# A two-layer attention and FFN kernel whose beginning is laid out anew and whose second-layer rows are laid in pairs

## The chip, the core and the metric

The kernel runs on one core of a Trainium2 chip. The metric is the device time of one execution in microseconds (us). The engines are TensorE (PE, with its weight loads as PEld), VectorE (DVE), ScalarE (ACT), GpSimd (POOL) and SyncE (SP), which issues all DMA transfers here.

## The reference

```python
def _A_ref(x, wq, wk, wv, wo):            # H = 32 query heads, one key/value head, Dh = 16
    q = (x @ wq).reshape(B, S, H, Dh).transpose(0, 2, 1, 3)
    k = x @ wk
    v = x @ wv
    scores = jnp.einsum("bhqd,bkd->bhqk", q, k) * (Dh ** -0.5)
    p = softmax(scores, axis=-1)
    o = jnp.einsum("bhqk,bkd->bhqd", p, v)
    return o.transpose(0, 2, 1, 3).reshape(B, S, H * Dh) @ wo

def _B_ref(x, w1, w2):
    return jnp.maximum(x @ w1, 0) @ w2

for _ in range(2):                        # the same weights in both layers
    x = x + _A_ref(layernorm(x), wq, wk, wv, wo)
    x = x + _B_ref(layernorm(x), w1, w2)
```

x is 1 x 2048 x 512 in float32, w1 is 512 x 1792 and w2 is 1792 x 512. The layer norm has no gain and no offset.

## The kernel before, in words

The 2048 positions are four blocks of 512. The attention of a layer is cut into 32 units; a unit (U) is one block of 512 queries with four of the 32 heads, and runs over 16 tiles of 128 keys. One unit and one key tile make a step, so that both layers together have 1024 steps. A step is two pairs of score matmuls on PE (`scores`, L788, each with 64 of the 128 rows, two side by side), two exponentials on ACT of 128 x 1024 (L789), and eight value matmuls (`values`, L794). After its last tile a unit's sums are kept (L801, L803), stored, and read back in another layout (`unit_out` L810, `unit_sums` L817 and L819), inverted and spread through DRAM (`unit_inverse` L831, L833), and scaled (`unit_norm` L842).

The matrix products run on fp16 halves of float32 numbers: a product of two numbers is three products of high and low halves (`projection`, `mm3` L104; `batch` L125 uses 64 rows for two products side by side). A layer norm is L269 and L271 (statistics, DVE), L272 and L273 (variance to scale, POOL), L278 (apply, DVE); `halved` makes its fp16 high half on DVE (L287) and its low half on DVE or POOL (L288); `laid` transposes both by a DMA (L294) into a home, a tile that holds a block's 512 normed and transposed rows. `transposed` does the same on PE (L301).

`keys` (L315) makes the keys and values of one block: 12 products, a copy out of PSUM by `high` (L97 on ACT when the work is forced, L99 on DVE when not), two casts (L323), and the subtractions for the low parts on DVE and POOL (L325). The last block of a set also finds the key maximum, `key_norm`, whose row goes into the key tile by two DMAs (L355). `query` makes the queries of eight heads of one block (a group): it stores a high, a low and again a high half, for the upper and the lower 64 partitions each, into a DRAM buffer `qd` (L401). `squares` stores a row of squared lengths for every unit, in two DMAs a group (L381). `load_q` reads a unit's query tile from there (L749), and five such tiles turn over. The zero rows of the key and query tiles are written once, by ACT (L181) or POOL (L183).

All dense work besides the steps (norms, keys, queries, out-projection, FFN) stands in a queue of generators, each with a size and a step by which it is due. A planner, `timed`, walks through the 1024 steps with costs for scores, exponentials and values, and puts pieces of the first generator between them at a rate of size by steps left. A generator can yield ("lag", ..) to leave time for a result. `until` runs the queue at once until a condition holds: the work is then forced. `CHAINS` gives for each block the size and the due step of its out-projection and FFN. The first 32 steps take units 0 and 1 in turn, four key tiles each, so that key block b is needed from step 8b on. Layer 2 starts at step 512, and needs the keys of blocks 0 to 2 and the key maximum from there; its first ten units take tiles 12 to 15, those of block 3, in a second pass.

`start` (L410) normalises the first four tiles of rows and transposes them on PE, then makes the queries of group 0, then keys, then the squares. The other 12 tiles follow one at a time, laid by DMA, and block by block keys and a query group. `others` (L477) makes the queries of blocks 1, 2 and 3 later. In `chain` (L576) the down-projection of the FFN calls `finish` (L728) for each tile of 128 rows; for layer 1 it makes the norms for layer 2, and after all four the rows are laid together, followed by keys(1, b) and the list `fill` of query batches and squares that go into later gaps; `rest` (L706) empties that list.

## Time and profile before

| what | before |
|---|---|
| median of 3 runs | 2550.78 us (2549.84 to 2554.6) |
| profiled execution | 2550.61 us |
| its span | 2548.8 us |
| PE busy | 2376.9 us, 93% |
| ACT busy | 1974.4 us, 77% |
| DVE busy | 664.7 us, 26% |
| POOL busy | 241.1 us, 9% |
| mean granted TensorE clock | 0.977 |

In rows of groups of instructions, a line, an engine, an operation and the tiles (output <- input) are followed by the shapes, the count, the busy time in us, the mean in ns, and the idle time before them with what ended it. In rows of the timeline stand the start in us, the length, the engine, the line, the operation, the count of such instructions in a row, and in brackets the idle time before and what released it. SPq is a DMA issued by SP. A row of a stretch gives its limits and length, then the busy time and count of each engine.

### The profile page before, as it was taken

Reading aid. Unit: us, or ns where it says so; the run is one execution under the profiler, and the core shown is the slowest. Engines: PE = TensorE matmul, PEld = TensorE weight load, DVE = VectorE, ACT = ScalarE, POOL = GpSimd, SP = SyncE. Lnnn points to the kernel's source line nnn. Section 1 sums busy time; section 2 is a strip of 40 time slices with the busy share of each in tenths; the row PEclk is TensorE's granted clock in tenths of the full one; section 3 lists DMA queues with packets and bytes.
Section 4 is the critical chain, followed back from the end, with each engine's and each line's share of the span. In section 5 each row is a group of like instructions: output and inputs, shape, how many; then the busy total and the mean of one; then the engine's idle time right before and its main releaser. Section 6 shows DMA issues by size and latency. Waiting matters only on the chain.

```text
span 2548.8 us, 44836 instructions
## 1 busy us (share of the span) xinstructions
PE 2376.9 (93%) x18965; PEld 790.2 (31%) x18965; DVE 664.7 (26%) x1482; ACT 1974.4 (77%) x2090; POOL 241.1 (9%) x289
## 2 busy tenths in 40 slices
PE   5699999999999988999799998979999999999978
PEld 1122222333233323333133332223333333233334
DVE  4333322111421233222221122232123111221232
ACT  5489998888888876777588787868888888888720
POOL 3434520000100011000110000000000000000000
PEclk9899999999999999999899999999999999999989
DMA  3334432110321122210231112321122111121131
GB/s 105 91 112 152 127 113 69 57 58 17 94 90 57 41 78 54 95 54 30 73 87 40 44 38 65 122 82 57 41 71 74 53 57 54 54 71 44 35 117 64
DMA packets 168356, 180.78 MB, mean 71 GB/s; under 512 B 78956, under 2 KB 98684, under 8 KB 167632
## 3 DMA queue, kind: packets, MB, share of 16 engines
q1 hardware_dynamic: 168144, 177.81, 22.8%
q8 instruction: 150, 2.46, 0.4%
q14 instruction: 62, 0.51, 0.1%
HBM read 115.06 MB, written 47.97 MB: 64 GB/s over the span
## 4 chain that ended last, share of the span: by engine, by line
PE 77%; ACT 9%; DMA 4%; DVE 4%; issue 3%; POOL 2%; SPq 1%; ACTq 0%; POOLq 0%; DVEq 0%
PE facc L794 33%; PE fmisc L125 22%; PE fst L788 17%; ACT fp L789 8%; PE fmisc L104 4%; DMA fqd<-fqh 1%; DMA fod<-faccs 1%; DVE fxt L555 1%; DVE fbst L269 1%; SPq L401 1%; DMA flsum<-fod 1%; DMA frinv<-frd 0%; POOL fbmv L273 0%; POOL fxp L288 0%; DMA frd<-flsum 0%
## 5 line engine op out<-in xcount | busy, mean ns | idle before, releaser
L789 ACT ACTIVATE fp<-fst 128x1024 f32<-128x1024 f32 x2048 | 1943.8, 1029 | 420.2 <-PE fst L788 401.6
L794 PE MATMUL facc<-fp,fva 128*32 128x512 f32 x8192 | 1030.4, 605 | 5.1 <-DVE faccs L801 4.1
L788 PE MATMUL fst<-fqop,fkop 64*128 64x512 f16 x4096 | 790.2, 383 | 55.3 <-ACT fp L789 35.9
L788 PEld LDWEIGHTS <-fkop 64*128 64x128 f16 x4096 | 262.7, 93 | 865.7 <-issue 696.7
L794 PEld LDWEIGHTS facc<-fp,fva 128*32 128x32 f32 x8192 | 208.7, 108 | 411.0 <-issue 361.6
L125 PE MATMUL fmisc<-fw,fhh 64*128 64x512 f16 x1568 | 258.1, 376 | 5.4 <-DVE fseen L132 3.6
L555 DVE SCALAR_TENSOR_TENSOR fxt<-fmisc,fxt 128x512 f32<-128x512 f32 x156 | 102.5, 682 | 367.1 <-PE fmisc L125 343.8
L125 PE MATMUL fmisc<-fxt,fw 64*128 64x512 f16 x1344 | 188.2, 376 | 1.9 <-DMA fw<-fwd 0.8
L272 POOL TENSOR_SCALAR fbmv<-fbmv 128x1 f32<-128x1 f32 x64 | 17.8, 278 | 1782.2 <-DVE fbmv L271 1781.3
L132 DVE COPY fseen<-fmisc 1x1 f32<-1x1 f32 x266 | 28.4, 142 | 552.4 <-PE fmisc L125 552.1
L125 PEld LDWEIGHTS <-fw 64*128 64x128 f16 x2352 | 118.5, 94 | 128.5 <-issue 22.5
L125 PE MATMUL fmisc<-fxq,fw 64*128 64x512 f16 x1008 | 141.2, 377 | 11.5 <-DMA fxq<-fxp 11.0
L125 PE MATMUL fmisc<-fw,fhl 64*128 64x512 f16 x784 | 151.7, 376 | 0.0
L646 DVE TENSOR_SCALAR fhh<-fmisc 128x512 f16<-128x512 f32 x98 | 67.1, 685 | 295.1 <-PE fmisc L125 295.1
L125 PEld LDWEIGHTS <-fhh 64*128 64x128 f16 x1568 | 80.7, 94 | 78.9 <-issue 15.5
L801 DVE COPY faccs<-facc 128x512 f32<-128x512 f32 x64 | 44.2, 690 | 225.2 <-PE facc L794 225.2
L647 DVE SCALAR_TENSOR_TENSOR fhl<-fmisc,fhh 128x512 f16<-128x512 f32 x112 | 77.4, 691 | 35.3 <-ACT fhh L644 31.9
L125 PE MATMUL fmisc<-fwoh,fot 64*128 64x512 f16 x448 | 78.2, 376 | 2.5 <-DVE fseen L132 1.6
L516 POOL TENSOR_SCALAR faccs<-faccs 128x512 f32<-128x512 f32 x32 | 48.9, 1528 | 65.7 <-DVE fw L515 52.0
L125 PE MATMUL fmisc<-fxq,fwqh 64*128 64x512 f16 x320 | 52.9, 376 | 0.0
L397 POOL TENSOR_TENSOR fsq<-fqh 128x512 fp32r<-128x512 f16 x32 | 33.3, 1039 | 201.2 <-DVE fqh L99 195.2
L125 PEld LDWEIGHTS <-fhl 64*128 64x128 f16 x784 | 40.5, 94 | 36.1
(124 smaller groups left out, 995.7 us busy)
## 6 DMA issues: line engine op xcount, KB each, us to landing
fw<-fwd SPq DMA_DIRECT2D x224, 256.0 KB
fod<-faccs SPq DMA_DIRECT2D x64, 256.0 KB
fqop<-fqd SPq DMA_DIRECT2D x148, 98.0 KB
fxt<-in_A_x_dram SPq DMA_DIRECT2D x32, 256.0 KB
fqd<-fqh SPq DMA_DIRECT2D x128, 64.0 KB
foraw<-fod SPq DMA_DIRECT2D x32, 256.0 KB
frinv<-frd SPq DMA_DIRECT2D x32, 256.0 KB
faccs<-in_B_w_dram SPq DMA_DIRECT2D x28, 256.0 KB
```

The source lines that it names most:

```text
L104: self.nc.tensor.matmul(ps, a, b, start=(i == 0), stop=(i == n - 1))
L125: mm(ps[j], a[r], b[r], start=(turn == 0 and i == 0), stop=(turn == 1 and i == n - 1), skip_group_check=True)
L132: self.nc.vector.tensor_copy(self.wt("seen", [1, 1]), t[0:1, 0:1])
L397: nc.gpsimd.tensor_mul(sq[G], _f(qh), _f(qh))
L516: nc.gpsimd.tensor_scalar(raw, raw, self.ws, None, op0=MUL)
L555: self.nc.vector.scalar_tensor_tensor(xt, ps, 1.0 / factor, xt, op0=MUL, op1=ADD)
L646: nc.vector.tensor_scalar(hh, ps, 0.0, None, op0=MAX)
L647: nc.vector.scalar_tensor_tensor(hl, ps, 0.0, _f(hh), op0=MAX, op1=SUB)
L788: nc.tensor.matmul(st[:, hf], self.kop[U // 32][h, kt * P:(kt + 1) * P], q[h, pr, :], start=True, stop=True)
L789: nc.scalar.activation(p[:, 2 * pr:2 * pr + 2], st, AF.Exp, scale=self.up ** -2)
L794: self.nc.tensor.matmul(acc[32 * j:32 * j + 32], self.va[U // 32][:, kt], p[:, 2 * pr + hf], start=start, stop=stop, skip_group_check=True)
L801: self.nc.vector.tensor_copy(self.sums[U], acc)
```

## The change

1. `begin` takes the place of `start` for this path. Eight row tiles are loaded at the beginning, the last four behind the query weights. The order on PE is transposes of the rows, keys, the first query group, the key transposes and maximum, the squares. Zero rows are written by DVE; those of the later query tiles and of layer 2's key tile are put at step 5 (`remaining`).
2. The layer norms of tiles 4 to 7 stand right behind `begin`, those of tiles 8 to 15 at steps 1, 3, 7 and 9 (`rows`), in pairs and not one at a time; of each pair one low half is made on DVE, the other on POOL. Four homes hold the four blocks: xt2, xq2, ot2 and wo2, so that one block instead of two goes through DRAM (`xtd`). `following` then holds only keys and queries of blocks 1 to 3, and its keys are copied by DVE. `others` takes the blocks in the order 1, 3, 2; the out-projection weights, whose tile is a home now, come after that.
3. `qd` has another layout: `query` stores 3 tiles of 128 partitions in place of 6 of 64; `squares` stores all groups of a block with 2 DMAs in place of 8; a query load reads 49 x 2 x 512 in place of 49 x 1024 elements.
4. In layer 1 each pair of rows is laid in `finish`; the squares that are left in `fill` go before the last down-projection; for blocks 0 and 1 the first query batch follows the keys at once; the lag ahead of the keys is 8 throughout; the sizes and due steps of blocks 0 and 2 are other numbers.
5. The tile of the unit's outputs and of its spread inverse are double; units 33, 35 and 37 are scaled 14 steps behind and not 8.

```diff
-CHAINS = (((397, 272), (449, 400), (449, 508), (421, 626)), ((384, 784), (384, 912), (384, 1022), (384, 1152)))
+CHAINS = (((421, 272), (449, 400), (425, 500), (421, 626)), ((384, 784), (384, 912), (384, 1022), (384, 1152)))
...
             for h in (32, 96):
-                if early:
+                if not self.exact:
+                    self.nc.vector.memset(flat[h:h + 32], 0.0)
+                elif early:
...
-        r = 8 * len(groups)
-        nc.vector.tensor_scalar(qr[0:r], ps[0:r], 2 * SLACK / ONE, None, op0=MUL)
-        for i, G in enumerate(groups):
-            for pr in range(2):
-                nc.sync.dma_start(self.qd[L, b][2 * G:2 * G + 2, :, 48, pr, :].rearrange("u h q -> (u h) q"),
-                                  _f(qr)[8 * i + pr * 4:8 * i + pr * 4 + 4])
+        nc.vector.tensor_scalar(qr, ps[0:32], 2 * SLACK / ONE, None, op0=MUL)
+        n, G = 4 * len(groups), groups[0]
+        for pr in range(2):
+            dst = self.qd[L, b][G:G + len(groups), pr, :, :, 48].rearrange("g u h q -> g (u h) q")
+            nc.sync.dma_start(dst, _f(qr)[16 * pr:16 * pr + n])
...
-            for pr in range(2):
-                for c, t in ((0, qh), (1, ql), (2, qh)):
-                    dst = qd[2 * G:2 * G + 2].rearrange("u h (c d) p q -> c p (u h) d q", d=DH)[c, pr]
-                    nc.sync.dma_start(dst, _f(t)[64 * pr:64 * pr + 64])
+            for c, t in ((0, qh), (1, ql), (2, qh)):
+                dst = qd[G, :, :, :, c * DH:(c + 1) * DH].rearrange("p u h d q -> (p u h) d q")
+                nc.sync.dma_start(dst, _f(t))
...
+    def begin(self):
...
+        st = {t: self.stats(self.xin[t]) for t in range(2)}
+        xn = {0: self.apply(*st[0])}
+        self.prep_wkv(kraw)
+        for t in range(4):
+            if t < 2:
+                st[t + 2] = self.stats(self.xin[t + 2])
+            if t < 3:
+                xn[t + 1] = self.apply(*st[t + 1])
+            yield from self.transposed(xn[t], t, self.xt2)
+            self.load_x(t + 8)
+        self.prep_wq(qraw)
...
+        keys = self.keys(0, 0, self.xt2)
+        for w in keys:
+            yield w
+            if isinstance(w, tuple):
+                break
+        queries, squares = self.in_parts(0, 0, [0], self.xt2)
+        yield from queries
+        yield from keys
+        yield from squares
+
+    def rows(self, n):
+        while self.row < n:
+            todo, t = [], self.row
+            self.row += 2
+            for r in (t, t + 1):
+                self.ln(self.xin[r], r, todo)
+            for xp, r in todo:
+                self.laid(xp, r % 4, self.homes()[r // 4])
...
+    def remaining(self):
+        self.zero_rows(self.qop[2:] + [self.kop[1]])
+        self.fixed_rows(self.qop[2:] + [self.kop[1]])
+        self.nc.gpsimd.memset(self.va[1], self.vs / self.os)
+
+    def following(self):
+        yield ("lag", 1, 0.0, 9.0)
+        for b in range(1, NB):
+            self.rows(4 * b + 4)
+            yield from self.keys(0, b, self.homes()[b])
+            if b == 2:
+                self.nc.sync.dma_start(self.xtd, self.ot2[2])
+            yield from self.queries(0, 0, [b])
...
+        if L == 0 and b < NB - 1 and not self.exact:
+            yield from self.rest(fill)
+            fill = []
         yield from down(ready)
...
-            to = self.xq2 if b < NB - 1 else self.xt2
-            if b < NB - 1:
-                yield from self.rest(fill)
-                fill = []
-            for xp, r in self.todo:
-                self.laid(xp, r, to)
-            self.todo.clear()
-            yield ("lag", 1, 0.0, 4.0 if 0 < b < NB - 1 else 8.0)
-            yield from self.keys(1, b, to)
-            self.fill = fill + self.in_parts(1, b, range(4), to)
+            yield ("lag", 1, 0.0, 8.0)
+            yield from self.keys(1, b, self.row_home(b))
+            self.fill = fill + self.in_parts(1, b, range(4), self.row_home(b))
+            if b < 2:
+                yield from self.fill.pop(0)
...
             self.ln(xt, s, self.todo)
+            if s % 2:
+                for xp, r in self.todo:
+                    self.laid(xp, r, self.row_home(b))
+                self.todo.clear()
...
+            self.until(lambda: not self.gens)
+            self.rows(8)
+            self.add(self.following(), 80, 24)
             self.add(self.others(), 156, 142)
-            self.until(lambda: self.tile_no >= 5)
...
+            for i, t in ((1, 10), (3, 12), (7, 14), (9, 16)):
+                at(i, self.rows, t)
+            at(5, self.remaining)
...
-                    inverse, norm = (3, 6) if U == 31 else (5, 8) if 32 < U < 40 else (7, 12) if U % 8 == 7 else (9, 14)
+                    inverse, norm = (3, 6) if U == 31 else (7, 12) if U % 8 == 7 else (9, 14)
```

Three places show the instructions' order. The first is SP's queue at the beginning, from the first query stores (fqd) to the last key row; fqop are query tiles, fkop_75 is layer 1's key tile, fqr a row of squares or of the key maximum. Before:

```order
L401 DMA fqd_94<-fqh 4x16x512
L401 DMA fqd_94<-fql 4x16x512
L401 DMA fqd_94<-fqh 4x16x512 x2
L401 DMA fqd_94<-fql 4x16x512
L401 DMA fqd_94<-fqh 4x16x512
L381 DMA fqd_94<-fqr 4x512 x2
L749 DMA fqop_88<-fqd_94 49x1024 x2
L749 DMA fqop_89<-fqd_94 49x1024 x2
L355 DMA fkop_75<-fqr 1x4x512 x2
```

And of the change:

```order
L403 DMA fqd_93<-fqh 8x16x512
L403 DMA fqd_93<-fql 8x16x512
L403 DMA fqd_93<-fqh 8x16x512
L359 DMA fkop_75<-fqr 1x4x512 x2
L385 DMA fqd_93<-fqr 4x512 x2
L822 DMA fqop_87<-fqd_93 49x2x512 x2
L822 DMA fqop_88<-fqd_93 49x2x512 x2
L298 DMA_TRANSPOSE fxq<-fxp 128x8x128 x2
```

The six stores are three, and the key row stands ahead of the squares and of the query loads.

The second is DVE's queue ahead of the keys of block 1. Before (fkv, a block's keys and values, is there copied by ACT):

```order
L269 BN_STATS fbst<-fxt 128x6
L271 BN_AGGR fbmv<-fbst 128x2
L278 TENSOR_SCALAR fxn<-fxt,fbmv 128x512
L287 CAST fxp<-fxn 128x512
L801 COPY faccs<-facc 128x512 x2
L323 CAST fkop_75<-fkv 48x512 x2
L325 TENSOR_TENSOR fkop_75<-fkv,fkop_75 16x512
```

And of the change, the last of four pairs of norms and what follows it:

```order
L282 TENSOR_SCALAR fxn<-fxt,fbmv 128x512 x2
L291 CAST fxp<-fxn 128x512
L292 TENSOR_TENSOR fxp<-fxn,fxp 128x512
L291 CAST fxp<-fxn 128x512
L179 MEMSET fqop_89 32x512 x2
L179 MEMSET fqop_90 32x512 x2
L179 MEMSET fqop_91 32x512 x2
L179 MEMSET fkop_76 32x1024 x2
L99 COPY fkv<-fmisc 128x512
L327 CAST fkop_75<-fkv 48x512 x2
L329 TENSOR_TENSOR fkop_75<-fkv,fkop_75 16x512
```

The zero fills and the copy of fkv stand on DVE now; L287 has become L291, L288 L292, L323 L327 and L325 L329.

The third is SP's queue at the end of layer 1's block 2, from the stores of the FFN's results (fxr) to layer 2's last key row, with the query stores between them (9 rows of them are left out at ...). Before:

```order
L734 DMA fxr_104<-fxt 128x512 x4
L401 DMA fqd_99<-fqh 4x16x512
L401 DMA fqd_99<-fql 4x16x512
...
L381 DMA fqd_99<-fqr 4x512 x8
L294 DMA_TRANSPOSE fxq<-fxp 128x8x128 x4
L355 DMA fkop_76<-fqr 1x4x512 x2
```

And of the change:

```order
L822 DMA fqop_91<-fqd_97 49x2x512 x2
L883 DMA fod<-faccs 128x512
L385 DMA fqd_98<-fqr 4x4x512 x2
L803 DMA fxr_103<-fxt 128x512 x2
L298 DMA_TRANSPOSE fxq<-fxp 128x8x128 x2
L803 DMA fxr_103<-fxt 128x512 x2
L298 DMA_TRANSPOSE fxq<-fxp 128x8x128 x2
L359 DMA fkop_76<-fqr 1x4x512 x2
```

The query stores stand elsewhere, further ahead; two square stores, of the whole block each, stand ahead of the rows, and the four transposes are two times two.

More of the change, by code (lines that the diff above doesn't have):

```diff
@@ L171, in setup, with zero_rows @@
             self.wms = self.ct("wms", [P, 4, NF, 2])
-            self.xtd = [self.dp.tile([P, 2, 4, D], F16, name=f"fxtd{b}") for b in range(NB)]
+            self.xtd = self.dp.tile([P, 2, 4, D], F16, name="fxtd")
             self.wd = [self.dp.tile([NF, P, 2, D], F16, name=f"fwd{i}") for i in range(2)]
-    def zero_rows(self, tiles, early):
+    def zero_rows(self, tiles, early=False):
         for t in tiles:
@@ L258, in w @@
             return lambda: self.split(m, f, raw, False)
-        out = [lambda c=c: wo(c) for c in range(4)]
-        if not self.exact:
-            out += [lambda m=m, f=f: w(m, f) for f in range(NF) for m in range(2)]
-        return out
+        out = [] if self.exact else [lambda m=m, f=f: w(m, f) for f in range(NF) for m in range(2)]
+        return out + [lambda c=c: wo(c) for c in range(4)]
     def stats(self, xt):
@@ L440, in start @@
                 load(t + 6)
-            self.tile_no = t
-            to = self.xt2 if b == 0 else self.xq2 if b == 1 and not self.exact else self.ot2
-            if self.exact or self.solo:
-                yield from self.transposed(xn[t], t % 4, to)
-            else:
-                self.laid(self.halved(xn[t], nc.gpsimd), t % 4, to)
+            yield from self.transposed(xn[t], t % 4, self.ot2 if b else self.xt2)
             yield ("lag", 0, 0.0, 2.4)
@@ L461, in start @@
             elif t % 4 == 3:
-                if not self.exact and b > 1:
-                    nc.sync.dma_start(self.xtd[b], to[2])
-                yield ("lag", 0, 0.0, 1.6 if self.exact else 4.0)
-                yield from self.keys(0, b, to)
+                yield ("lag", 0, 0.0, 1.6)
+                yield from self.keys(0, b, self.ot2)
                 yield from self.queries(0, 0, [b])
+    def begin(self):
+        nc = self.nc
+        self.xin, self.row = {}, 4
+        for t in range(4):
+            self.load_x(t)
+        kraw, qraw = self.load_wkv(), self.load_wq()
+        for t in range(4, 8):
+            self.load_x(t)
+        zero = self.ident[0:2, 2:3].to_broadcast([2, P])
+        nc.vector.tensor_scalar(self.crow[:, 0], zero, ONE, None, op0=ADD)
+        nc.vector.tensor_scalar(self.crow[:, 1], zero, -ONE, None, op0=ADD)
+        self.zero_rows([self.kop[0]])
+        self.fixed_rows([self.kop[0]])
+        st = {t: self.stats(self.xin[t]) for t in range(2)}
+        xn = {0: self.apply(*st[0])}
+        self.prep_wkv(kraw)
+        for t in range(4):
+            if t < 2:
[5 more added lines that the diff above has]
+        self.prep_wq(qraw)
+        self.zero_rows(self.qop[0:2])
+        self.fixed_rows(self.qop[0:2])
+        self.late_consts()
+        keys = self.keys(0, 0, self.xt2)
[7 more added lines that the diff above has]
+        yield from squares
@@ L992, in run @@
         self.outs = self.asked = 0
+        self.ol = {}
         self.fill = []
         self.setup()
-        self.add(self.start(), 200 if self.exact else 176, 29)
+        self.add(self.start() if self.exact else self.begin(), 200, 29)
         steps, self.loaded = self.order(), 0
```

54 lines of the change are left out of this document (33 added, 21 removed).

## The prediction

> **What bounds the kernel now.** I read the page first: the span, the engines, the granted clock and the costliest groups.
>
> ```profile
> span 2548.8 us, 44836 instructions
> ...
> PE 2376.9 (93%) x18965; PEld 790.2 (31%) x18965; DVE 664.7 (26%) x1482; ACT 1974.4 (77%) x2090; POOL 241.1 (9%) x289
> ...
> PEclk9899999999999999999899999999999999999989
> ...
> L789 ACT ACTIVATE fp<-fst 128x1024 f32<-128x1024 f32 x2048 | 1943.8, 1029 | 420.2 <-PE fst L788 401.6
> L794 PE MATMUL facc<-fp,fva 128*32 128x512 f32 x8192 | 1030.4, 605 | 5.1 <-DVE faccs L801 4.1
> L788 PE MATMUL fst<-fqop,fkop 64*128 64x512 f16 x4096 | 790.2, 383 | 55.3 <-ACT fp L789 35.9
> ```
>
> TensorE (PE) is busy for 93% of 2548.8 us. One of the 1024 attention steps costs it 4 x 383 ns of scores in two concurrent pairs and 8 x 605 ns of values in concurrent fours; by the groups' busy time that is (790.2 + 1030.4) / 1024 = 1.78 us, against 2 x 1.03 us of exponentials on ACT. With the dense work added, PE sets the pace nearly everywhere, at a granted clock that reads 9 in nearly every slice; an edit pays only in a stretch in which PE stalls. I therefore asked for the busy times and instruction counts by stretch, with an undisturbed one (1540 to 1560) as a yardstick. Behind the length stand PE, its weight loads, DVE, ACT and POOL, each with its count, then the granted clock, the DMA share and GB/s.
>
> ```profile
> 60.00:140.00 80.00, 56.00 (x297) 14.64 (x297) 31.71 (x60) 38.02 (x40) 32.75 (x35) 0.85 0.30 76
> ...
> 940.00:980.00 40.00, 26.84 (x178) 7.21 (x172) 8.66 (x16) 20.41 (x22) 3.43 (x3) 0.83 0.34 96
> ...
> 1220.00:1260.00 40.00, 22.24 (x119) 5.86 (x115) 7.68 (x16) 14.00 (x16) 3.64 (x3) 0.71 0.23 58
> 1540.00:1560.00 20.00, 20.00 (x166) 5.43 (x162) 2.27 (x5) 19.62 (x22) 0.00 (x0) 1.00 0.08 26
> 1580.00:1620.00 40.00, 31.25 (x224) 7.36 (x223) 10.79 (x26) 26.79 (x29) 2.08 (x2) 0.87 0.30 99
> ```
>
> The yardstick does 166 PE records in 20 us. The stretch 60 to 140 has 297, about 36 us of work, and holds 80: some 40 us are lost there, with ACT at 40 instructions in 80 us. By the same rule 940 to 980 (178 records, a dozen of them slower full-row products, 23 us) loses 17; 1220 to 1260 (119, about 15 us) loses 25; 1580 to 1620 (224, 27 us) loses 13. The change touches all four places. Other losses, at the out-projections and at the end, it leaves alone. The profiled execution took 2550.61 us, 1.8 us of it outside the span, and the median of the runs shown is 2550.78, so a sum against the one holds for the other.
>
> **The start.** The first 32 steps take each block of 512 keys as soon as it exists: steps 0, 8, 16 and 24 need blocks 0, 1, 2 and 3. These rows of the timeline show the query loads, the first scores, and the scores that the next three blocks release.
>
> ```profile
> 33.01 1.30 SPq L749 DMA_DIRECT2D fqop<-fqd  x4
> ...
> 38.65 1.23 PE L788 MATMUL fst<-fqop,fkop 64*128 64x512 f16 x4 [4.70 <-DMA fkop<-fqr]
> ...
> 60.76 1.56 POOL L325 TENSOR_TENSOR fkop<-fkv,fkop 16x512 f16<-16x512 f32 x1 [16.47 <-DVE fkop L323]
> ...
> 62.37 0.39 PE L788 MATMUL fst<-fqop,fkop 64*128 64x512 f16 x1 [0.63 <-POOL fkop L325]
> ...
> 93.22 0.39 PE L788 MATMUL fst<-fqop,fkop 64*128 64x512 f16 x1 [0.63 <-POOL fkop L325]
> ...
> 128.47 0.60 ACT L97 ACTIVATE fkv<-fmisc 128x512 f32<-128x512 f32 x1 [13.70 <-issue]
> ...
> 131.76 0.60 PE L788 MATMUL fst<-fqop,fkop 64*128 64x512 f16 x3 [0.63 <-POOL fkop L325]
> ```
>
> Block 1 is there at 62.4, block 2 at 93.2, block 3 at 131.8 us. The first scores at 38.65 wait for the last key row (L355), which stands in SP's queue behind six query stores, two square rows and four query loads. In the new order that row is ahead of the squares and the loads, but the loads stay the last link; on the other side keys come ahead of queries on PE, and three stores replace six. I take a first score at 38, a gain of 0.6, with 36.5 and 39.5 as bounds.
>
> In the changed kernel block 1 waits for VectorE (DVE): its copy of keys and values (L99) stands behind four pairs of layer norms, a copy of values and eight zero fills. What a DVE instruction of a pair costs, undisturbed and in the first 140 us:
>
> ```profile
> L269 DVE BATCH_NORM_STATS2 fbst<-fxt 128x6 f32<-128x512 f32 x2 | 1.4, 694 | 0.1
> ...
> L278 DVE TENSOR_SCALAR fxn<-fxt,fbmv 128x512 f32<-128x512 f32 x2 | 1.1, 531 | 0.7 <-POOL fbmv L273 0.7
> ...
> L288 DVE TENSOR_TENSOR fxp<-fxn,fxp 128x512 f16<-128x512 f32 x1 | 0.7, 691 | 0.0
> ...
> L287 DVE CAST fxp<-fxn 128x512 f16<-128x512 f32 x1 | 0.4, 421 | 0.0
> ```
>
> ```profile
> L278 DVE TENSOR_SCALAR fxn<-fxt,fbmv 128x512 f32<-128x512 f32 x16 | 12.9, 807 | 2.0 <-POOL fbmv L273 2.0
> ...
> L287 DVE CAST fxp<-fxn 128x512 f16<-128x512 f32 x12 | 7.4, 625 | 0.0
> L183 POOL MEMSET fqop<- 32x1024 f16 x6 | 6.4, 1059 | 0.3
> ...
> L183 POOL MEMSET fkop<- 32x2048 f16 x2 | 3.6, 1798 | 0.1
> ...
> L104 PE MATMUL fmisc<-fxq,fwkh 128*128 128x512 f16 x8 | 2.4, 384 | 0.0
> ```
>
> A pair is two each of L269 (0.69), L278 (0.53) and L287 (0.42), one L288 (0.69), and two short aggregates that I put at 0.2: 4.4, with the 0.7 wait for the variance 5.0 us; four pairs 20. From the end of the key work near 31.5 that is 51.5; the value copy 0.7. For a DVE zero fill of 32x512 words there is no row. From below it is the 0.42 of L287, a cast that long, twice that for 32x1024: 6 x 0.42 + 2 x 0.84 = 4.2. From above POOL's own 1.06 and 1.80: 10.0. I take the one-operand 0.53 of L278, which has the same engine and length: 6 x 0.53 + 2 x 1.06 = 5.3. Then the copy of the keys, 0.7 like L288, two casts like L287, 0.84, and POOL's 16 rows, 1.56 as at 60.76: 61 us. So block 1 gains little: DVE sets it.
>
> Blocks 2 and 3 gain. Their rows are now all laid by step 9, so they are no longer made one tile at a time between blocks, and ACT's copy at 128.47, which had stood 13.70 behind other work, is DVE's. What remains between blocks is PE's work: eight steps (8 x 1.78 = 14.2), 12 key products and as many for a query group (24 x 0.384 = 9.2), transposes and squares 1: 24.5 us, where now 30.8 and 38.5 pass. Block 2 is there at 86, block 3 at 110 less what PE does ahead while it waits for block 1, some 2: 108. Gain 131.8 - 108, about **23** us. From below: fills at 10.0 and disturbed rows (next paragraph) put block 1 near 70, block 3 at 119, a gain of 13. From above: 20 us a block, that is 16 exponentials of 1.03 and a few us, gives 101 and a gain of 31.
>
> In the first 140 us L278 takes 807 ns and L287 625, against 531 and 421 alone: 0.97 us more in each pair, while POOL works on the same rows. The change moves half of POOL's low parts to DVE, and the rest stays. The Trainium skill ("SBUF — State Buffer", section "SBUF: two separate sides") says that the two engines lock a port pair against each other for a whole instruction. That agrees with these rows and speaks against the half that stays on POOL. If the whole excess remained, four pairs would add 3.9 us to block 1, and the start would gain 19 in place of 23; that is inside the bounds.
>
> **The ends of blocks, second layer's rows.** Up to now four rows' transposes go to SP together, behind eight square stores. At block 1:
>
> ```profile
> 948.71 5.00 SPq L381 DMA_DIRECT2D fqd<-fqr  x8
> ...
> 954.12 5.46 SPq L294 DMA_TRANSPOSE fxq<-fxp  x4
> ...
> 961.58 1.01 PE L104 MATMUL fmisc<-fxq,fwkh 128*128 128x512 f16 x2 [10.78 <-DMA fxq<-fxp]
> ```
>
> SP spends 5.00 us on eight square stores and 5.46 on four transposes, and PE waits 10.78 for them. With two stores (5.00 x 2 / 8) 3.75 us fall away; with two transposes sent a batch earlier another 2.7: 6.5 straight off this wait, the lower bound. The squares, moved ahead of the last FFN batch, and the queries that the new list starts right behind the keys give PE work beneath the rest. Upper bound 15, all but 2 of the 17 lost; I take **13**, nearer the top, since PE has waited for a transfer and not for arithmetic.
>
> At the end of block 2, layer 2 cannot begin without that block's keys:
>
> ```profile
> 1230.51 4.02 SPq L381 DMA_DIRECT2D fqd<-fqr  x8
> ...
> 1234.62 5.41 SPq L294 DMA_TRANSPOSE fxq<-fxp  x4
> ...
> 1241.95 1.01 PE L104 MATMUL fmisc<-fxq,fwkh 128*128 128x512 f16 x2 [10.27 <-DMA fxq<-fxp]
> ...
> 1251.14 0.37 PE L348 MATMUL fmisc<-fident,fkmx 128*1 128x128 f32 x1 [2.52 <-DVE fkmx L346]
> ...
> 1254.26 1.70 PE L788 MATMUL fst<-fqop,fkop 64*128 64x512 f16 x4 [2.74 <-DMA fkop<-fqr]
> ```
>
> Stores and transposes give 4.02 x 6/8 + 5.41/2 = 5.7. Here the key part starts at step 509 to 511 and not when forced at 512, so three steps (5.3 us) cover the wait. The records of this stretch (119 for 22.24 busy) show 7 us of slow clock, 0.71 granted, which follows the idle time; I count 6 back. Sum **17**. What stays is 2.52 and 2.74 us of the key maximum and its row. Bounds: 10 (clock not regained) and 21 (25 lost less 4 of these waits). Block 0 goes the same way earlier, with cover; I count nothing.
>
> Around 1580 the same eight stores delay a unit's inverse on SP:
>
> ```profile
> 1572.27 4.82 SPq L381 DMA_DIRECT2D fqd<-fqr  x8
> ...
> 1577.18 0.34 SPq L831 DMA_DIRECT2D frd<-flsum  x1
> ...
> 1582.96 0.69 DVE L842 TENSOR_TENSOR foraw<-foraw,frinv 128x512 f32<-128x512 f32 x1 [7.58 <-DMA frinv<-frd]
> ...
> 1585.01 1.03 PE L125 MATMUL fmisc<-fxt,fwqh 64*128 64x512 f16 x4 [6.13 <-DVE fseen L132]
> ```
>
> The inverse is stored at 1577.18, right behind the stores (1572.27 + 4.82); DVE waits 7.58 for its return, in order, and PE 6.13 behind a DVE flag. The stores' end comes 3.6 us earlier, and the normalisation of these units moves from 8 to 14 steps behind, some 12 us, which covers 7.58. Gain **9**, between 4 (the stores alone) and 13 (all of the loss).
>
> **The rest.** The larger query stores take SP issues away where SP is not waited for; cover: 5 query buffers. Weights of the out-projection formed later, double buffers for the normalised outputs: nothing, beneath PE's work. The loads of queries now read pieces half as long. One took:
>
> ```profile
> 113.24 2.39 DMA fqop<-fqd
> ```
>
> 2.39 us. It is issued more than a unit's 16 steps (16 x 1.78 = 28 us) ahead, so nothing; without that cover, see the third rival.
>
> Sum 23 + 13 + 17 + 9 = 62: 2550.6 - 62 = **2488** us. Lower bounds 13 + 6.5 + 10 + 4 = 33.5 give 2517; upper 31 + 15 + 21 + 13 = 80 give 2471.
>
> **The rivals.** First: the start gains nothing, because DVE is the bound there. Block 1 at 70 and then 31 us a block, as block 2 needs now, bring block 3 at 132 again. For it: DVE takes four pairs, fills and copies into one queue. Against: after block 1 only two pairs are left. It gives 2550.6 - 39 = 2512.
>
> Second: the ends of blocks gain nothing, the rows being late for their own sake (the last pair's norm, landing) and not for SP's queue. For it: the waits 10.78 and 10.27 end with the landing of a transpose. Against: SP was issuing for all of that time. Only the start is gained: 2528.
>
> Third, slower: query loads in twice as many, half-size pieces. If a landing took twice its 2.39 us and every unit waited half of a landing more (64 x 1.2 = 77), the loss would be over the gain: 2550.6 - 62 + 77 = 2565. It decides from 0.97 us a unit on. Against: the landing has 28 us of lead; for it: the many small pieces on the queues at the same places as the weight loads.
>
> Fourth: it does not do what it says; the places are freed and the time turns up behind them as the next wait on ACT or PE, within 5 us of now: 2550.
>
> **How the numbers follow.** The forecast has 0.68; the first rival 0.11, the second 0.10, the third 0.08, the fourth 0.03. A measurement of this kernel can tell about 0.2%, 5 us, from no change. Faster: 0.68 + 0.11 + 0.10 = 0.89; the same 0.03; slower 0.08. The forecast's own range is 2471 to 2517; it is taken down to 2468 and up to 2528, so that the first two rivals lie within it.
>
> **What would show it.** Right: the scores of blocks 2 and 3 start near 86 and 108; PE's waits for transposed rows near 950 and 1230 fall below 4 us, and layer 2 starts about 53 us earlier; no wait of DVE for the returned inverse at layer 2's first units. Wrong at the start: a DVE queue without gaps up to 70 and key copies late for blocks 2 and 3 too. Wrong at the ends: PE still waits some 10 us for a transpose while SP is idle. The third rival shows as PE or ACT waiting for query tiles at the first steps of units, all over the run.

## The result and the profile after

| | before | changed |
|---|---|---|
| median | 2550.93 us (2549.84 to 2554.6, 4 runs) | 2505.41 us (2503.12 to 2506.58, 4 runs) |
| ratio | 1 | 0.9818, 95% interval 0.9801 to 0.9835 |
| span of the profiled execution | 2548.8 us | 2501.3 us |

The change makes the kernel 45.5 us faster, where 62 were forecast. From the page of the changed kernel:

```profile
span 2501.3 us, 44680 instructions
...
PE 2366.6 (95%) x18965; PEld 792.2 (32%) x18965; DVE 675.3 (27%) x1507; ACT 1965.4 (79%) x2080; POOL 221.7 (9%) x275
```

Of the 47.5 us by which the span is shorter, 10.3 are PE's busy time (2366.6 against 2376.9 us) and the rest is idle time. To see where it went, I took from each trace the time at which the first exponential of a step ends. The columns behind the second give how much earlier than before that was, for the changed kernel and for three kernels of the experiments below.

| step | before, us | changed | before + new stores | changed + old stores | last version |
|---|---|---|---|---|---|
| 0 | 40.5 | 3.3 | 1.6 | 1.3 | 5.8 |
| 24 | 133.3 | 17.5 | 4.4 | 13.9 | 20.6 |
| 32 | 151.5 | 18.9 | 4.4 | 14.0 | 20.5 |
| 384 | 910.0 | 13.5 | 4.6 | -3.7 | 17.5 |
| 410 | 984.4 | 19.6 | 11.0 | 1.0 | 32.5 |
| 508 | 1223.3 | 18.2 | 10.8 | -7.1 | 31.5 |
| 512 | 1256.7 | 35.5 | 15.6 | 10.3 | 46.9 |
| 640 | 1555.8 | 35.1 | 14.7 | 9.9 | 45.6 |
| 680 | 1648.8 | 47.7 | 26.2 | 17.0 | 58.8 |
| 704 | 1719.1 | 46.3 | 28.1 | 16.6 | 74.7 |
| 1023 | 2434.0 | 48.0 | 28.2 | 18.3 | 70.1 |

One trace is one execution. Four kernels of the experiments whose first 32 steps are those of the changed kernel had leads from 15.6 to 19.0 us at step 32, so differences of up to 3.4 us in this table say nothing.

The start, from the timeline (L385 and L822 of the changed kernel are L381 and L749 of before; L861 are scores, L867 values):

```profile
34.87 1.67 PE L861 MATMUL fst<-fqop,fkop 64*128 64x512 f16 x4 [8.07 <-DMA fqop<-fqd]
...
61.56 0.60 PE L861 MATMUL fst<-fqop,fkop 64*128 64x512 f16 x1 [0.41 <-POOL fkop L329]
...
90.81 0.39 PE L861 MATMUL fst<-fqop,fkop 64*128 64x512 f16 x1 [0.63 <-POOL fkop L329]
...
114.30 0.39 PE L861 MATMUL fst<-fqop,fkop 64*128 64x512 f16 x1 [0.63 <-POOL fkop L329]
```

The first scores came at 34.87 (38.65 before), block 1 at 61.56 (62.37), block 2 at 90.81 (93.22), block 3 at 114.30 (131.76). Groups of DVE's instructions in the first 140 us (L282 and L291 are L278 and L287 of before):

```profile
L282 DVE TENSOR_SCALAR fxn<-fxt,fbmv 128x512 f32<-128x512 f32 x16 | 8.9, 559 | 5.1 <-POOL fbmv L277 5.1
...
L291 DVE CAST fxp<-fxn 128x512 f16<-128x512 f32 x12 | 5.0, 420 | 0.0
...
L179 DVE MEMSET fqop<- 32x512 uint32 x10 | 4.8, 485 | 1.6 <-issue 1.6
...
L179 DVE MEMSET fkop<- 32x1024 uint32 x4 | 3.6, 912 | 1.1 <-issue 1.1
```

A zero fill takes 0.49 us, 0.91 for the double size, and the norms' instructions 559 and 420 ns, where it had been 807 and 625. The stretches between blocks 1 and 2 and between 2 and 3:

```profile
61.50:91.00 29.50, 23.73 (x126) 5.97 (x126) 14.93 (x33) 15.92 (x16) 8.04 (x13) 0.88 0.32 86
...
91.00:114.50 23.50, 20.11 (x126) 5.58 (x125) 6.93 (x14) 15.92 (x16) 2.62 (x2) 1.00 0.12 35
```

Both hold 126 PE records and 16 ACT instructions. The one takes 29.5 us at a granted clock of 0.88, the other 23.5 at 1.00.

The ends of blocks 1 and 2, the waits for the transposed rows and for the key maximum:

```profile
926.92 4.65 SPq L298 DMA_TRANSPOSE fxq<-fxp  x2
...
933.63 1.01 PE L104 MATMUL fmisc<-fxq,fwkh 128*128 128x512 f16 x2 [6.36 <-DMA fxq<-fxp]
...
1206.19 0.61 PE L104 MATMUL fmisc<-fxq,fwkh 128*128 128x512 f16 x2 [0.66 <-DMA fxq<-fxp]
...
1215.95 0.27 PE L352 MATMUL fmisc<-fident,fkmx 128*1 128x128 f32 x1 [2.05 <-DVE fkmx L350]
...
1218.95 1.55 PE L861 MATMUL fst<-fqop,fkop 64*128 64x512 f16 x4 [2.73 <-DMA fkop<-fqr]
```

At block 1 PE still waits 6.36 us (10.78 before), at block 2 0.66 (10.27). Of the waits as a whole (sum, times, longest) these matter below:

```profile
DVE foraw L915 <- DMA frinv<-frd: 49.6, 12, 7.8
...
PE fmisc L125 <- DMA fxq<-fxp: 11.0, 1, 11.0
...
PE fmisc L104 <- DMA fxq<-fxp: 7.0, 2, 6.4
```

DVE's waits for the spread inverse (first row) were 27.5 us in 7 turns in the kernel before: with the change they grew.

### The profile page after: what moved, and what is told of

The parts are those of the page before. It is cut to its first block, busy times and chain, and to the rows that moved or that the text cites. A ratio compares the mean times of both kernels' runs of the same rounds, so it can differ in the third digit from the quotient of the medians.

```text
span 2501.3 us, 44680 instructions
## 1 busy us (share of the span) xinstructions
PE 2366.6 (95%) x18965; PEld 792.2 (32%) x18965; DVE 675.3 (27%) x1507; ACT 1965.4 (79%) x2080; POOL 221.7 (9%) x275
## 4 chain that ended last, share of the span: by engine, by line
PE 76%; ACT 12%; DVE 5%; DMA 3%; issue 2%; POOL 2%; SPq 1%; ACTq 0%; POOLq 0%; DVEq 0%
PE facc L867 33%; PE fmisc L125 22%; PE fst L861 17%; ACT fp L862 12%; PE fmisc L104 4%; DVE fxt L622 1%; DVE fbst L273 1%; DMA frd<-flsum 1%; DMA frinv<-frd 1%; POOL fbmv L277 0%; DMA fxq<-fxp 0%; DVE fxp L291 0%; PE fmisc L378 0%; POOL fxp L292 0%; DVE fxp L292 0%
## 5 line engine op out<-in xcount | busy, mean ns | idle before, releaser
L867 PE MATMUL facc<-fp,fva 128*32 128x512 f32 x8192 | 1025.3, 603 | 4.1 <-DVE faccs L874 3.6
L861 PE MATMUL fst<-fqop,fkop 64*128 64x512 f16 x4096 | 791.7, 382 | 54.0 <-ACT fp L862 31.8
L861 PEld LDWEIGHTS <-fkop 64*128 64x128 f16 x4096 | 263.5, 93 | 864.8 <-issue 704.6
L867 PEld LDWEIGHTS facc<-fp,fva 128*32 128x32 f32 x8192 | 209.3, 108 | 409.7 <-issue 363.0
L125 PE MATMUL fmisc<-fwo,fot 64*128 64x512 f16 x672 | 95.9, 376 | 2.0 <-DVE fseen L132 1.8
L125 PEld LDWEIGHTS <-fhl 64*128 64x128 f16 x784 | 41.2, 94 | 36.5
L711 ACT ACTIVATE fhh<-fmisc 128x512 f16<-128x512 f32 x14 | 8.4, 597 | 51.6 <-PE fmisc L104 51.6
```

Source lines behind the costliest of these rows:

```text
L125: mm(ps[j], a[r], b[r], start=(turn == 0 and i == 0), stop=(turn == 1 and i == n - 1), skip_group_check=True)
L861: nc.tensor.matmul(st[:, hf], self.kop[U // 32][h, kt * P:(kt + 1) * P], q[h, pr, :], start=True, stop=True)
L867: self.nc.tensor.matmul(acc[32 * j:32 * j + 32], self.va[U // 32][:, kt], p[:, 2 * pr + hf], start=start, stop=stop, skip_group_check=True)
```

## The experiments

The theory after these rows: the row of SP's instructions and the planner's placing set the time at the ends of blocks; the start is set by DVE up to block 1, and by PE behind it. The rivals: pair-wise laying alone does it; the square stores do it; a DVE queue that is late all through the start.

**The old stores in the changed kernel.** The layout of `qd`, `query`, `squares`, `load_q` as before.

```diff
-            for c, t in ((0, qh), (1, ql), (2, qh)):
-                dst = qd[G, :, :, :, c * DH:(c + 1) * DH].rearrange("p u h d q -> (p u h) d q")
-                nc.sync.dma_start(dst, _f(t))
+            for pr in range(2):
+                for c, t in ((0, qh), (1, ql), (2, qh)):
+                    dst = qd[2 * G:2 * G + 2].rearrange("u h (c d) p q -> c p (u h) d q", d=DH)[c, pr]
+                    nc.sync.dma_start(dst, _f(t)[64 * pr:64 * pr + 64])
...
```

> The changed kernel (2505) with the query and square stores and the DRAM layout as before: six stores of 64 partitions a group, eight square stores a block, loads in 2 KB pieces. If the eight stores ahead of the transposes were what cost the time at the ends of blocks, as the forecast's sum counts them (3.75 + 3.0 + 3.6 us, and about 1 at the start), this is 11 us slower: 2516. If moving the squares ahead of the last down-projection already took them out of the way, only the start and the stretch near 1550 lose: 2505 to 2510. If the half-size pieces of the loads cost something, it is faster than 2505.

Measured: 2533.06 us, ratio 0.9935 (0.9921 to 0.9949). That is 28 us more than the changed kernel, far more than any of the cases expected. By the table the loss comes in pieces: 4.9 by step 32 (not far above what two executions differ by), 12 more by step 384, 8 by step 508, and 5 around step 680. Two of the places, in this kernel's timeline (L404 are query stores, L905 stores an inverse, L907 loads it spread, L594 loads weights):

```profile
174.21 0.69 DVE L916 TENSOR_TENSOR foraw<-foraw,frinv 128x512 f32<-128x512 f32 x1 [11.75 <-DMA frinv<-frd]
...
177.87 1.94 PE L868 MATMUL facc<-fp,fva 128*32 128x512 f32 x8 [6.24 <-DVE faccs L875]
...
1026.37 0.94 SPq L404 DMA_DIRECT2D fqd<-fql  x1
...
1027.98 0.42 SPq L905 DMA_DIRECT2D frd<-flsum  x1
...
1032.22 0.67 SPq L907 DMA_DIRECT2D frinv<-frd  x1
...
1032.93 3.84 SPq L594 DMA_DIRECT2D fw<-fwd  x8
...
1036.67 0.61 PE L125 MATMUL fmisc<-fxt,fw 64*128 64x512 f16 x1 [3.63 <-DMA fw<-fwd]
```

At 1026 SP is still busy with the last of twelve query stores; only then does it store the inverse, wait for that to land, and load it (1032.22). The eight weight loads stand behind that wait, and PE waits 3.63 for them. At 174 DVE has waited 11.75 for a spread inverse; the copy of a unit's sums stands behind it on DVE, and PE's value matmuls wait 6.24 for that. The changed kernel at the same place:

```profile
155.33 0.57 SPq L403 DMA_DIRECT2D fqd<-fqh  x1
...
165.34 0.69 DVE L915 TENSOR_TENSOR foraw<-foraw,frinv 128x512 f32<-128x512 f32 x1 [7.79 <-DMA frinv<-frd]
...
169.00 1.07 PE L867 MATMUL facc<-fp,fva 128*32 128x512 f32 x8 [2.28 <-DVE faccs L874]
```

There it is 7.79 and 2.28. A store of 128 partitions takes SP 0.57 us (first row). The stores of 64, from the kernel before, take the same:

```profile
1562.48 0.55 SPq L401 DMA_DIRECT2D fqd<-fqh  x1
...
1569.56 0.52 SPq L401 DMA_DIRECT2D fqd<-fqh  x1
```

So what a query store costs here is SP's time per issue, nearly the same for half the partitions, and everything that waits behind it in order: 192 of them at medians of 0.52 and 0.55 us in this kernel, 96 at 0.57 and 0.59 in the changed one. The square stores are less even, from 0.31 us each for two of 4 rows (at 30.16 in the changed kernel) to 0.66 each for two of 16 rows (at 901.94).

**The new stores in the kernel before.** The same edit the other way round, and nothing else of the change.

> The kernel before (2549 to 2551), with the new layout of the DRAM buffer, three query stores a group, two square stores a block and loads in 1 KB pieces, and nothing else of the change. If SP's queue is the cause, in that six or twelve stores of some 0.57 us each stand ahead of a unit's inverse and of the weight loads and transposes behind it, this alone gives 15 to 28 us: 2523 to 2536. If the stores count only as the forecast had them (3.75 + 3.0 + 3.6 us, and under 1 at the start), 2540. If the stores matter only in the new order, 2545 to 2551.

Measured: 2523.96 us, ratio 0.9897 (0.9877 to 0.9917), 27 us less than before: the first alternative. Its rows at the ends of blocks 1 and 2 (L382 are squares, L295 transposes):

```profile
941.92 1.30 SPq L382 DMA_DIRECT2D fqd<-fqr  x2
...
943.32 5.39 SPq L295 DMA_TRANSPOSE fxq<-fxp  x4
...
950.80 1.01 PE L104 MATMUL fmisc<-fxq,fwkh 128*128 128x512 f16 x2 [4.62 <-DMA fxq<-fxp]
...
1226.59 1.01 PE L104 MATMUL fmisc<-fxq,fwkh 128*128 128x512 f16 x2 [5.72 <-DMA fxq<-fxp]
```

The transposes begin at 943.32 and not 954.12, of which 4.6 us are the lead from the start and 6.2 are the shorter row of stores (3.7 for the squares, 5.00 against 1.30, the rest for the query stores ahead of them); PE waits 4.62 and not 10.78. At block 2 it waits 5.72 and not 10.27. Behind step 640 another 13.5 us fall away, with units 33, 35 and 37 still scaled 8 steps behind as before.

**Eight square stores, three query stores.**

```diff
-        for pr in range(2):
-            dst = self.qd[L, b][G:G + len(groups), pr, :, :, 48].rearrange("g u h q -> g (u h) q")
-            nc.sync.dma_start(dst, _f(qr)[16 * pr:16 * pr + n])
+        for i, G in enumerate(groups):
+            for pr in range(2):
+                dst = self.qd[L, b][G, pr, :, :, 48].rearrange("u h q -> (u h) q")
+                nc.sync.dma_start(dst, _f(qr)[16 * pr + 4 * i:16 * pr + 4 * i + 4])
```

> The changed kernel (2503 to 2505), with eight square stores a block and three query stores a group. It divides the 28 us that the old stores cost it. If the query stores are the larger part, being twelve a batch ahead of the inverse and the weights, 2506 to 2512. If the eight square stores are, as the forecast thought, 2515 to 2530.

Measured: 2504.8 us, ratio 0.9821 (0.9805 to 0.9838), the changed kernel's time. The square stores cost nothing in the new order, in which they stand ahead of the last down-projection; the 28 us belong to the query stores, or to the 2 KB pieces of the loads that go with their layout, which no run takes apart. The traces speak against the loads: PE's waits that name a query tile are 10.0 us with the old stores and 8.1 in the changed kernel, and the DMA engines' busy share is 22.5% and 23.0%.

**The rows laid together.**

```diff
-            if s % 2:
-                for xp, r in self.todo:
-                    self.laid(xp, r, self.row_home(b))
-                self.todo.clear()
...
+            for xp, r in self.todo:
+                self.laid(xp, r, self.row_home(b))
+            self.todo.clear()
             yield ("lag", 1, 0.0, 8.0)
```

> The changed kernel, but the four rows of a block are laid together after the last norm, as before. If laying in pairs is what brings the transposes early, the waits of PE for transposed rows at 927 and 1206 grow by two issues of 1.4 to 2.3 us and their landing, 3 to 5 us each, 2513 in all, with a wait of 4 us or more at 1206 where it is 0.66 now. If only the last pair decides, nothing changes: 2503 to 2508.

Measured: 2515.6 us, ratio 0.9872 (0.9857 to 0.9887), 10 us more. But the place is another: steps 256 to 288, the end of block 0, lose 9.5 of it.

```profile
629.95 5.95 SPq L298 DMA_TRANSPOSE fxq<-fxp  x4
...
637.89 1.01 PE L104 MATMUL fmisc<-fxq,fwkh 128*128 128x512 f16 x2 [7.57 <-DMA fxq<-fxp]
```

PE waits 7.57 us there, where the changed kernel has no such wait. At block 1 PE waits 8.22 and not 6.36, and at block 2 0.8 where 4 or more were expected; between steps 508 and 512 nothing more is lost. Why it is block 0 that needs the pairs, no run shows.

**The chains' old numbers.**

```diff
-CHAINS = (((421, 272), (449, 400), (425, 500), (421, 626)), ...
+CHAINS = (((397, 272), (449, 400), (449, 508), (421, 626)), ...
```

> The changed kernel, with the sizes and due steps of the four chains of layer 1 as before: (397, 272) and (449, 508) for blocks 0 and 2. If the earlier due step (500) is what brings the keys of block 2 ahead of step 512, layer 2 starts 8 to 12 us later and the end is as much later: 2512 to 2517. If the squares ahead of the last down-projection and the laying in pairs do it, the start of layer 2 stays within 3 us and the time at 2503 to 2508.

Measured: 2525.06 us, ratio 0.989 (0.9874 to 0.9907), 20 us more than the changed kernel. Against its trace 16 us are lost between steps 288 and 384, up to 25 by step 396; some comes back, and steps 508 to 512 lose 7.1. There PE waits again for the rows of block 2:

```profile
1232.06 1.03 PE L104 MATMUL fmisc<-fxq,fwkh 128*128 128x512 f16 x2 [3.44 <-DMA fxq<-fxp]
```

The 3.44 stands against 0.66. The direction was right and the size was not. The edit sets two blocks' numbers back at once, and most of the loss comes between steps 288 and 396, where no single long wait of PE stands behind it. A likely reason, not taken apart here, is that the sizes are what the planner paces by, and that a chain which holds a query batch more than its number says is pressed at its end.

**A longer lag ahead of block 1's keys.**

```diff
-            yield ("lag", 1, 0.0, 8.0)
+            yield ("lag", 1, 0.0, 16.0 if b == 1 else 8.0)
             yield from self.keys(1, b, self.row_home(b))
```

> The changed kernel, with a lag of 16 in place of 8 ahead of the second layer's keys of block 1, so that the planner puts about four more steps of attention ahead of them. If the PE wait of 6.36 us at 927 and the slower clock behind it (0.83 granted) are only a planner's error, both go: 5 to 7 us faster, 2499. If the attention steps without dense work between them only run at ACT's pace and the time comes back behind, 2503 to 2506.

Measured: 2498.11 us, ratio 0.9792 (0.9778 to 0.9805), against 0.9818 of the changed kernel; the intervals overlap by 0.0004, and the trace shows the place.

```profile
929.42 5.12 SPq L298 DMA_TRANSPOSE fxq<-fxp  x2
...
939.07 0.11 PEld L104 LDWEIGHTS <-fwkh 128*128 128x128 f16 x2 [0.84 <-DMA fqop<-fqd]
```

PE comes to the keys at 939.07 with nothing to wait for (the wait named, 0.84, is the weight load's). Between steps 396 and 404 this kernel gains 12 us on the changed one, and gives 5 back up to step 512. So the 6.36 us were the planner's: a lag of 8 ends before rows that are issued behind other transfers have landed.

**The zero fills later.**

```diff
-            at(5, self.remaining)
+            at(17, self.remaining)
```

> The changed kernel, with the eight zero fills and their constants at step 17 and not 5, behind block 2's keys. If DVE's queue sets block 1 (61.6 us), the 6.1 us of fills (52.1 to 58.2) go, block 1 is there at 55.5 and the end is 5 to 6 us earlier: 2500. If PE or ACT or the next norms take the time back, block 1 is earlier but block 3 stays near 114 and the time near 2505.

Measured: 2504.8 us, ratio 0.9828 (0.9814 to 0.9842), no change. Blocks 1 and 2 are 3.7 and 5.0 us earlier by the table's measure, block 3 is not (116.3 against 115.8). DVE sets block 1, as forecast, but the fills only move.

**Block 3's norms later.**

```diff
-            for i, t in ((1, 10), (3, 12), (7, 14), (9, 16)):
+            for i, t in ((1, 10), (3, 12), (12, 14), (14, 16)):
```

> The changed kernel, with the last four tiles of block 3 normed at steps 12 and 14 and not 7 and 9. If block 2 (90.8 us, 29.3 behind block 1) is late because two pairs of norms stand on DVE ahead of the copy of its queries (65.8 to 75.4), the interval falls to 25 and the end of the first 32 steps comes 3 to 5 us earlier, 2500 to 2502. If the norms only move to block 3's interval, block 2 is earlier, block 3 not, and the time is 2503 to 2507.

Measured: 2508.24 us, ratio 0.983 (0.9813 to 0.9846). Block 2 is no earlier (92.9 against 92.3), since another wait of PE takes the place of the one on the squares:

```profile
87.35 0.68 DVE L99 COPY fkv<-fmisc 128x512 f32<-128x512 f32 x1
...
88.08 1.12 PE L333 MATMUL fmisc<-fident,fkv 128*128 128x128 f32 x4 [3.72 <-DVE fkv L99]
```

PE waits 3.72 for the copy of keys. The wait on the squares is gone, but the norms now stand ahead of that copy. This cure fails; whether DVE's queue alone makes block 2 late is not settled.

**The inverse issued by POOL.**

```diff
-        nc.sync.dma_start(rd.rearrange("h (c x) -> h c x", x=32), l[:, 1])
+        nc.gpsimd.dma_start(rd.rearrange("h (c x) -> h c x", x=32), l[:, 1])
...
-        nc.sync.dma_start(r, rd[:, None, :].to_broadcast([8, DH, D]))
+        nc.gpsimd.dma_start(r, rd[:, None, :].to_broadcast([8, DH, D]))
```

> The changed kernel, with the store of a unit's inverse and its spread load issued by POOL and not by SP. By the theory that SP's order is what delays the inverse and, by its wait for the store's landing (3 to 4 us), the loads behind it, DVE's waits for the spread inverse fall from 49.6 us in all to under 20, the value matmuls no longer wait for DVE near 166, and the time is 3 to 6 us less: 2498 to 2502. If what is left is the round trip through DRAM itself, 2503 to 2506. If POOL's own work is held up by its waits (row norms and low halves), 2508 or more.

Measured: 2527.12 us, ratio 0.9907 (0.989 to 0.9924), 22 us more: the third alternative.

```profile
156.51 0.90 POOL L904 DMA_DIRECT2D frd<-flsum  x1 [1.18 <-DVE flsum L902]
...
165.74 0.92 DVE L915 TENSOR_TENSOR foraw<-foraw,frinv 128x512 f32<-128x512 f32 x1 [7.32 <-DMA frinv<-frd]
...
POOL frinv L906 <- DMA frd<-flsum: 96.4, 32, 5.3
...
DVE foraw L915 <- DMA frinv<-frd: 81.4, 14, 13.1
```

The store of the same inverse in the changed kernel, issued by SP:

```profile
156.52 0.44 SPq L904 DMA_DIRECT2D frd<-flsum  x1
```

POOL waits 96.4 us in 32 turns for the store to land, 3.0 each, and DVE's waits for the inverse grow from 49.6 to 81.4 us. The way through DRAM takes 9.2 us from the store's start at 156.51 to DVE's at 165.74, against 8.8 us when SP issues it (156.52 to 165.34). So it is to be waited out later, not issued elsewhere.

**Versions.** The changed kernel with both lags: 16 as above, and an empty piece ahead of the lag behind an out-projection, which the forced advance had consumed, so that PE waited 10.98 us at 1622 for the rows of layer 2's first FFN.

```diff
-            yield ("lag", 1, 0.0, 8.0)
+            yield from (0.0, ("lag", 1, 0.0, 12.0 if L and b == 0 else 8.0))
```

> The changed kernel with the lag of 16 ahead of the second layer's keys of block 1, and with the lag ahead of the first FFN of layer 2 kept (an empty piece ahead of it, and 12 for that block): now the forced out-projection consumes that lag, and PE waits 10.98 us at 1622 for the transposed rows. If both are the planner's errors and the time does not come back, 6 us and another 8 to 10 us less: 2487 to 2492. If the FFN, due later by as much, is pressed elsewhere, 2495 to 2499.

Measured: 2497.17 us, ratio 0.979 (0.9774 to 0.9806): no more than the one lag. The rows' wait of 10.98 is gone, and a wait of the values for DVE's copy of sums took its place:

```profile
1627.77 2.79 PE L867 MATMUL facc<-fp,fva 128*32 128x512 f32 x12 [5.40 <-DVE faccs L874]
```

Ahead of that copy on DVE stand the second pair of norms and a unit's scaling. So the next version also scales 17 steps behind, has two row buffers, and block 3's norms later.

```diff
-        qr = self.wt("qr", [32, D], F16, bufs=1)
+        qr = self.wt("qr", [32, D], F16, bufs=2)
...
-                    inverse, norm = ... (7, 12) if U % 8 == 7 else (9, 14)
+                    inverse, norm = ... (7, 12) if U % 8 == 7 else (9, 17)
```

> The changed kernel with both lags of the run before this one, two buffers for the row of squares (the row waits now 2.58 us for the key row's transfer ahead of the first scores), block 3's norms at steps 12 and 14, and the scaling of a unit's outputs 17 steps behind and not 14, so that DVE does not wait for the inverse's round trip through DRAM. If DVE's waits for the spread inverse (49.6 us in all, 7.8 at most) are what stops the value matmuls near 166 and 231, 2497 falls by 2 for the buffers and 3 to 4 for the waits: 2489 to 2493. If not, 2494 to 2498.

Measured: 2488.08 us, ratio 0.9747 (0.973 to 0.9764). The gain of 9.1 us is a little over the first case's. Three edits are in it at once, so no share of any one is shown. Last, without the later norms:

> The version of the run before this one (2488) with block 3's norms back at steps 7 and 9. Those norms alone, put later, gave 2508 where the changed kernel has 2505. If they cost 3 to 4 us there because they stand ahead of block 3's keys, this is 2484 to 2486, with block 3 at 114 and not 116. If the difference was only between executions, 2487 to 2490.

Measured: 2482.62 us, ratio 0.9738 (0.9724 to 0.9751), clear of the changed kernel. Against the run before it the intervals overlap, so the norms' own share is not settled.

```profile
DVE foraw L915 <- DMA frinv<-frd: 18.2, 4, 6.7
```

DVE's waits for the inverse are 18.2 us and not 49.6, and no wait of PE for transposed rows is left among the larger ones. In the table 16 us are gained between steps 680 and 704, of which 4.6 come back by the end; that this is work put off would fit, but is not shown.

## Why the prediction was right, and where it was not

The time lies in the range and the sign was right. The number nearest to it is not the forecast's 2488, 17 us away, but the first rival's 2512, 7 us away; yet that rival's reason, a start that gains nothing, did not come true. The sum was 16.5 us too large: layer 2 started 35.5 us earlier, where 53 were forecast. And one term that was put at nothing holds more than half of the gain. With the stores as before the time is 2533, outside the range, so that it lies inside is in part luck.

**"The rest: the larger query stores take SP issues away where SP is not waited for ... nothing."** This step failed. The stores with their layout are worth 27 us alone, where the forecast had counted 10 for the squares among them, and 28 as the last edit, where the squares cost nothing. The forecast looked at the waits that name a transfer (transposes, inverse) and counted only the square stores next to them, 3.75, 3.0 and 3.6 us; the twelve query stores stood in front in the same queue, 0.5 to 0.6 us each. The row that showed it before was there: the stores from 1562.48 to 1569.56 stand ahead of the squares at 1572.27. The page's SP is not listed among the busy engines, which is how a full queue goes unseen.

**The start, 23 us.** Measured 17.5 at block 3 and 18.9 at step 32, 15.6 to 19.0 with the four kernels of the same beginning. Of that some 5 are the stores (4.4 in the kernel before, 4.9 lost by undoing them), so the new order is worth 11 to 15. Block 1 came within 0.6 us of its 61, from the DVE sum: 0.49 and 0.91 a fill against 0.53 and 1.06 taken. The first score, at 34.87, gained 3.8 and not 0.6, more than its bounds (36.5 to 39.5) allowed: the transfer that it waits for is now a query load, and no longer the key row behind it. Block 2 came 5 us late: PE had nothing to do for 2.81 us while the squares waited for DVE and POOL, and in two places it ran at half the clock.

```profile
62.00:64.00 2.00, 2.00 (x8) 0.41 (x11) 0.00 (x0) 1.73 (x2) 0.00 (x0) 0.50 0.00 0
...
80.00:82.00 2.00, 2.00 (x7) 0.41 (x6) 0.00 (x0) 1.15 (x2) 0.00 (x0) 0.50 0.49 153
...
78.05 0.19 PEld L378 LDWEIGHTS fmisc<-fsq,fsel 128*128 128x128 f32 x1 [3.72 <-POOL fsq L400]
...
79.47 0.61 PE L104 MATMUL fmisc<-fot,fwkl 128*128 128x512 f16 x1
...
82.89 0.39 PE L104 MATMUL fmisc<-fot,fwkl 128*128 128x512 f16 x1
```

The first two rows are stretches of 2 us, both at a granted clock of 0.50. The 3.72 is the weight load's wait; PE's own stop is 2.81 us, from 75.24 to 78.05. Behind it a full-row product takes 0.61 us, and 0.39 again at 82.89. The other slow place, at 62, lies behind a wait of 4.71 us for DVE's copy of block 1's keys (until 58.92). The Trainium skill ("TensorE: Matmul & The Clock Gate", section "HAM oscillation — how this bites in real kernels") has the clock fall behind PE gaps of more than about 3.4 us. The fall behind the 4.71 us agrees. The stop of 2.81 us is shorter than that figure, with two waits of 0.5 us in the 3 us ahead of it, and there the measurement decides. The block 2 to block 3 interval, 23.5 us, was forecast at 24.5. The 3.9 us by which four pairs would have stayed longer did not come: the norms' instructions run at nearly their undisturbed price, 559 and 420 ns against 531 and 421. This is no evidence against the port lock that the prediction named. Single instructions of the kernel before show where its excess came from:

```profile
106.36 1.16 POOL L288 TENSOR_TENSOR fxp<-fxn,fxp 128x512 f16<-128x512 f32 x1
...
106.71 1.10 DVE L278 TENSOR_SCALAR fxn<-fxt,fbmv 128x512 f32<-128x512 f32 x1
107.58 2.29 POOL L183 MEMSET fqop<- 32x1024 f16 x2
107.73 1.25 DVE L287 CAST fxp<-fxn 128x512 f16<-128x512 f32 x1
```

Seven of its sixteen L278 begin while POOL works on a low part of 128x512 and take 1.08 to 1.38 us; three of its twelve L287 begin while POOL fills zero rows and take 1.25; the other L287 take 0.41 to 0.42. So the casts' excess was the fills', and not the low parts', as the prediction read it. In the changed kernel the fills are DVE's, and POOL begins its low part only behind the pair's last cast (75.85 behind 75.35 + 0.42), so that no L282 or L291 of these pairs meets one. No run shows what they would cost if they met.

**Block 1's end, 13 us.** Against the trace of before the lead grows by 6.1 around it (steps 384 to 410). The lower bound, 6.5, is near what the stores alone gave in the old order (6.4), but there 3.7 came from the squares, as forecast, and the rest from the query stores and not from transposes sent in pairs. The step that failed is "PE has waited for a transfer", as if the wait had to go: the planner put the keys 8 us behind the norms, and the rows needed more. The longer lag gained 12 at the place.

**Block 2's end, 17 us.** Measured 17.3. The number was right, the reasons only in part. In the old order the stores give 4.8 of it. In the new order undoing the stores (17.4 between steps 508 and 512) or the pairs (17.1) loses nothing there, and the chains' old numbers lose 7.1. What gives the other 10 is open; the squares ahead of the last down-projection stand in all of these runs. What stays, 2.05 and 2.73 us for the key maximum, was forecast (2.52 and 2.74).

**Around 1580, 9 us.** Measured 12.6 between steps 640 and 680. The stores alone give 11.5 to 13.5 with the scaling unchanged, and the change without them 7.1. The later scaling did not cover DVE's wait for the inverse, as the forecast had it:

```profile
1567.84 0.69 DVE L915 TENSOR_TENSOR foraw<-foraw,frinv 128x512 f32<-128x512 f32 x1 [4.03 <-DMA frinv<-frd]
```

With another of 4.89 at 1593.94 this is as much as the 7.58 and 1.35 of before. What went is PE's wait of 6.13 behind it; the longest of that kind is now 1.2.

**Between the places** the lead falls from 18.9 at step 32 to 13.5 at step 384. The forecast had none of this. By step 96, ahead of the first FFN chain, 4.5 of these 5.4 us are gone: 2.2 between steps 48 and 56, where PE stops for the 2.28 us at 169, and 1.6 between steps 80 and 88, with a like stop of 1.33 at 232.81. The rest stays open.

**The rivals.** The start did gain, against the first. The second came near at block 1 alone, where PE still waits 6.36. Of the third, slower loads in half-size pieces, nothing shows: PE waits for a query tile once, 8.07 us at the first score, and the kernel before with these loads was 27 us faster. Block 0, at which nothing was counted, would lose 9.5 us without pairs.

## What to carry to other kernels

A queue that issues all transfers is an engine: list what stands ahead of each transfer that something waits for, back to the last idle moment, and price every row by the issue time that the trace shows, which the bytes did not tell here. A planner's pause must cover the time to landing; one that is too short, or that a forced stretch consumes, shows as a PE wait for a transfer though the transfer is not late by its own queue. When a stop is removed, look for the next one behind the same in-order engine before counting its whole length.

## What the runs showed of the hardware

SP's time for one query store was nearly the same for 64 and for 128 partitions, 0.55 and 0.57 us. The Trainium skill ("DMA: Bandwidth & Descriptors", section "Rules for kernel authors") advises one transfer of 128 partitions over two to disjoint halves; these runs put 27 us on the layout that allows it in this kernel. POOL as issuer of the inverse's round trip did not shorten it: 9.2 us from the store's start (156.51) to DVE's (165.74), and 8.8 by SP. In the kernel before, two of DVE's norm instructions were slowed where they met POOL's: L278 took 1.08 to 1.38 us beside a low part and 0.51 to 0.56 alone, L287 took 1.25 beside a zero fill and 0.42 alone; the statistics (L269) took 0.66 to 0.69 in both cases. And the granted clock fell to 0.50 behind a stop of PE of 2.81 us, with two short waits ahead of it.
